# A retention layer with two feed-forward layers: side work at the turn placed by a table, a block of layer 2 written as a sequence of steps

## The chip, the cores and the metric

The kernel runs on one core of a Trainium2 chip. The metric is the time of one execution on the device in microseconds (us). Three runs of the kernel before took 824.14, 824.81 and 824.89 us, a median of 824.81 us.

## What is computed

The reference is a retention attention (scores with a decay, no softmax), whose output is the input of a first feed-forward layer with a leaky rectifier and of a second one with an ELU:

```python
scores = q @ k.transpose / sqrt(64)            # 4 batches, 8 heads, 576 positions, 64 wide
x = (scores * Dmat) @ v                        # Dmat: gamma ** (i - j) for i >= j
x = x.reshape(2304, 512)
h = x @ moe_w_in                               # 512 -> 2048
x = np.maximum(0.01 * h, h) @ moe_w_out        # 2048 -> 512
h = x @ moe2_w_in
g = np.where(h > 0.0, h, np.exp(np.minimum(h, 0.0)) - 1.0)
return g @ moe2_w_out                          # (2304, 512), all float32
```

## The kernel before, in words

**Precision.** TensorE works on float32r operands. A float32 value is kept as a high part (ScalarE copies it to float32r) and a low part (value minus high part, a subtraction on VectorE, "DVE", or GpSimd, "POOL"), and a product is the sum of three: high by high, low by high, high by low. The weights arrive as 64-bit words and are rounded in the kernel. `split_a` issues two ScalarE ("ACT") passes, `split_b` (its generator is `split_ops`, lines 370 to 377) four DVE passes and then the next weight load, `split_c` the high part on ACT (line 388) and the low part on POOL or DVE (line 390). `raw` tiles are what arrives, `u` and `last` the words in work, `wih`, `wil`, `woh`, `wol` the parts of input and output weights.

**Tiling.** The 2304 tokens are four blocks of 512 and a small one of 256. The 2048 inner features are handled in four rounds q of four tiles of 128. Layer 1 is a list of 72 units n, one for a block, a round and one tile (the small block: two tiles). Unit n computes h on PE (`moe_h`, tag `ps_h`, four banks of PSUM), its activation in high and low part (`gh`, `g` on ACT, lines 432 and 433, `gl` on DVE, line 439; in the small block lines 462 to 477), and, three units later (`LAG`), the product with the output weights (`moe_y`, four banks `ps_y`). After a block's last tile of a round, `evac` (line 579, four DVE adds into `yp`; lines 522 and 523 for the small block) empties the four `ps_y` banks. The next block's `moe_y` writes the same four banks. The last round is n = 54 to 71; blocks 0 and 1 are emptied at n = 60 and 64, the small block at n = 66, block 2 at n = 70, block 3 inside layer 2.

**The turn.** Layer 2 computes its first product of a 512-token block by a scheme with seven half-size products instead of eight (`seventh`, numbered 1 to 7), for which the block's output is first turned into sums and differences (`stage`, a generator with nine calls of `side()`): seven ACT high parts (line 642), seven low parts (line 646), four to five DVE differences `t` (line 650), four stores to a scratch in HBM (line 656, `x<-xs`). `load_x` (line 689, `xo<-x`) reads them back as operands. Two of the four weight tiles of a round need sums of their own (`sums_a`: four POOL additions, lines 702 to 705; `sums_b`: line 714 on ACT, 715 on POOL, into `ws`). In the kernel before the place of all this is set by several rules in the loop over n: `begin(n)` and `may_split` start roundings in front of `moe_h`, `held`, `sums_a`, `sums_b`, and `load_x` stand at fixed n, and `side()` is called twice a unit.

**Layer 2.** `seven` is one 512-token block: the products in the order 1, 2, 5, 3, 6, 7, 4, sums of them on DVE (`add_up`, `c`, line 849) with copies on ACT (`copy_of`, `cc`, line 854), four ELU pieces (`elu`: ACT 747 and 749, DVE 751, high part ACT 755, low part DVE 757, into `gg`), one or two weight roundings, and at four places (`spot`) a fourth of an earlier block's output product (`second_y`). Round 0 is emptied by ACT (line 577), the later ones by DVE (line 579). `head = blk == 0` has an order of its own by conditions. The small block is `small_h` and `small_y`.

All engines take their instructions in the written order: this kernel is scheduled by hand. DMAs are issued by SP, in order too, each behind its waits.

Of the kernel before, what the change touches and what calls it, by code (L numbers as in the profile page):

```python
# [10 lines left out]
F32 = mybir.dt.float32  # L11
# [80 lines left out]
def retention_moe(  # L92
# [245 lines left out]


    sources = {"i": [w1_in, w2_in], "o": [w1_out, w2_out]}  # L340
    weights, raws, words = {}, {}, {}

    def load_w(key):
        kind, i = key
# [35 lines left out]
    def split_c(key):  # L380

        u = words[key]
        if key[0] == "o" or key[1] < FT:
# [228 lines left out]
        if loads:  # L612
            load_w(loads.pop(0))

    second = ("i", FT + 2)

    def may_split(n):

        if not splits or splits[0] not in raws or splits[0] == second:
            return False  # L620
        kind, i = splits[0]
        if i >= FT and n >= 63:
            return False
        return i < WB or last_use[kind, min(i, FT + 1) - WB] <= n + (kind == "i")


# [3 lines left out]
    def stage(blk):  # L630

        a = yp.pop(blk)
        n = SIZES[blk] // 2
# [48 lines left out]
        yield from pair(3, t4)  # L682
        yield
        send(3)
# [23 lines left out]
    def sums_b(key):  # L708
        i = key[1]
        for j in (i, i + 1):  # L710
            del words["i", j]
        t = sums[i]
        w = xpool.tile([P, 2, 4, DM // 2], F32R, tag="x", name="ws")
        nc.scalar.activation(w[:, 0], t, AF.Copy)
        nc.gpsimd.tensor_tensor(w[:, 1], t, w[:, 0].bitcast(F32), ALU.subtract)
        sums[i] = w
# [145 lines left out]
            go(steps)  # L862
        over.clear()

    def seven(q, blk, room, rounds, keep, side, begun=None):

        n = SIZES[blk] // 2
        to = (blk + 1) % NMAIN if (q, blk) != (NQ - 1, NMAIN - 1) else None  # L870
        r = list(rounds) + [None] * (2 - len(rounds))
        head = blk == 0
        g = []

        def fetch(k):
            if to is not None and (q, to) != (0, NMAIN - 1):
                load_x(to, k)

        finish()
        fetch(0)  # L880
        a = bank("h", 4)
        seventh(a, q, blk, 0, True)
        p1 = copy_of(a)
        if r[0]:
            split_a(r[0])
        b = bank("h", 4)
        seventh(b, q, blk, 1, True)
        fetch(1)
        c11 = add_up(b, p1)
        z = bank("h", 4)  # L890
        seventh(z, q, blk, 2, True)
        p5 = copy_of(z)
        e11 = elu(c11, g, 0, slice(0, n))
        go(e11, 2)
        if r[0]:
            split_b(r[0])
            load_next()
        spot()
        side()
        g.append(room())  # L900
        go(e11, 1)
        if r[1]:
            split_a(r[1])
        go(e11, 1)
        if begun:
            sums_b(begun)
        seventh(z, q, blk, 3)
        fetch(2)
        p53 = copy_of(z)
        seventh(a, q, blk, 4)  # L910
        c12 = add_up(a, p53)
        go(e11)
        side()
        if r[0] and not keep and not head:
            split_c(r[0])
        e12 = elu(c12, g, 0, slice(n, 2 * n))
        go(e12, 2)
        rest = split_ops(r[1]) if r[1] else iter(())
        if not head:
            go(rest, 3)  # L920
            go(e12, 1)
        spot()
        side()
        if r[0] and head:
            split_c(r[0])
        if not head:
            go(e12, 1)
        seventh(a, q, blk, 5)
        fetch(3)
        c22 = add_up(a, p5)  # L930
        go(e12, 1 + head)
        e22 = elu(c22, g, 1, slice(n, 2 * n))
        go(e22, 2)
        if not head:
            go(rest)
        go(e12)
        spot(2 if head and q > 0 else 1)
        go(rest)
        if r[1]:
            load_next()  # L940
        if r[1] and not keep:
            split_c(r[1])
        side()
        g.append(room())
        go(e22, 1)
        seventh(a, q, blk, 6)
        e21 = elu(a, g, 1, slice(0, n))
        go(e21, 2)
        go(e22, 1)
        go(e21, 1)  # L950
        over.extend((e22, e21))
        pending.append(second_y(q, blk, g))
        spot()

    with tc.manual_schedule():
        qk, v, k = slice(0, 2), slice(2, 3), slice(3, 4)
# [73 lines left out]
            while stages and next(stages[0], end) is end:  # L1030
                stages.popleft()

        held = [("i", FT + 2), ("i", FT + 3)]
        for n, u in enumerate(units):
            p = units[n - LAG] if n >= LAG else None
            if n == B * NMAIN:
# [10 lines left out]
            if n > 2:  # L1047
                begin(n)
            elif n == 0:
                att_q(nxt)  # L1050
# [1 line left out]
            moe_h(u)  # L1052
            for key in rounded:
                split_c(key)
            if n in (69, 70):
                split_c(held[n - 69])
            if rounded == [("i", FT + 1)]:
                sums_a(("i", FT))
            if n == 58:
                sums_b(("i", FT))  # L1060
            side()
            if n == 0:
                att_a(nxt, "h", 4)
                for a in range(1, B):
# [24 lines left out]
            side()  # L1089
            if n > 69:  # L1090
                side()
            for key, at in zip(held, (63, 64)):
                if n == at:
                    assert splits.pop(0) == key
                    split_a(key)
                elif n == at + 1:
                    split_b(key)
                    load_next()
            if n == 65:
                sums_a(held[0])  # L1100
            if n == 70:
                sums_b(held[0])
            if n in (66, 67, 71):
                load_x(0, (66, 67, 71).index(n))

        def first_y(p):
            moe_y(p)
# [7 lines left out]
        def room():  # L1115
            return hpool.tile([P, 2, 2, DM], F32R, tag="gg", name="gg")

        def last_block():
            yield
            yield from stage(NMAIN - 1)  # L1120

        load_x(0, 3)
        stages.append(last_block())
        for q in range(NQ):
            for blk in range(NB):
                if blk < NMAIN:
                    rounds = [splits.pop(0) for _ in range(min(2, len(splits)))]
                    held = rounds if blk == NMAIN - 1 else []
                    seven(q, blk, room if (q, blk) != (0, 0) else big_room, rounds, bool(held), side, begun if held else None)
# [94 lines left out]
```

## Time and profile before

| | |
|---|---|
| median of three runs | 824.81 us |
| profiled execution | 824.94 us |
| its span | 823.2 us |
| around the span | 1.7 us |
| TensorE clock granted, mean | 0.995 |
| PE busy in the span | 802.7 us, 98% |
| DVE, ACT, POOL busy | 531.7, 442.5, 178.7 us |
| layer 1, last round (n = 54 to 71) | about 343 to 445 us |
| layer 2, rounds 0 to 3 | from about 445 us |

PE is the engine that is nearly always busy. The idle time of the others is no loss by itself; the places to look at are those at which PE waits, and the clock that it is granted there.

### The profile page before, as it was taken

What the parts mean: (1) busy time and instruction counts of PE and PEld (TensorE: products, weight loads), DVE (VectorE), ACT (ScalarE), POOL (GpSimd) and SP (SyncE); (2) the same over time, 40 slices, a digit from 0 to 9 for tenths busy, and PEclk for the clock granted to TensorE, in tenths of its full rate; (3) what the DMA queues carried; (4) which work ended last, traced back from release to release, by engine and by line L of the source; (5) the groups of instructions that cost most, each with busy time, mean ns of one, the idle gap of its engine ahead of it and who ended that gap; (6) DMA issues with size and microseconds to landing.
All of it is one profiled execution on the core that took longest, in us unless ns stands there. A gap on an engine that the chain in (4) does not pass through costs nothing.

```text
span 823.2 us, 13324 instructions
## 1 busy us (share of the span) xinstructions
PE 802.7 (98%) x5240; PEld 712.9 (87%) x5240; DVE 531.7 (65%) x861; ACT 442.5 (54%) x755; POOL 178.7 (22%) x160
## 2 busy tenths in 40 slices
PE   9889999999999999999899999999999999999998
PEld 6778888888888888888678879889999999999997
DVE  5998952575244762678765677647776787666544
ACT  3466534554244532555535587777665676555442
POOL 2566431000000000032354123321133112320000
PEclk9999999999999999999899999999999999999999
DMA  9994520122000220122474976726653566545612
GB/s 340 323 335 139 191 78 14 51 78 78 1 25 26 77 77 1 51 76 85 173 261 176 385 277 256 245 76 268 235 218 137 200 263 246 187 131 179 227 53 77
DMA packets 34094, 129.97 MB, mean 158 GB/s; under 512 B 4080, under 2 KB 7408, under 8 KB 26736
## 3 DMA queue, kind: packets, MB, share of 16 engines
q1 hardware_dynamic: 33744, 128.99, 43.8%
q8 instruction: 41, 0.67, 0.3%
q14 instruction: 21, 0.17, 0.1%
q10 hardware_dynamic: 288, 0.14, 0.1%
HBM read 109.71 MB, written 19.40 MB: 157 GB/s over the span
## 4 chain that ended last, share of the span: by engine, by line
PE 37%; DVE 5%; ACT 5%; DMA 3%; issue 1%; POOL 1%; SPq 0%; DVEq 0%; ACTq 0%
PE ps_y L409 20%; PE ps_h L409 17%; DMA xo<-x 2%; DVE gg L757 1%; ACT cc L854 1%; ACT u L358 1%; DVE yp L579 1%; ACT last L360 1%; ACT gg L755 1%; DMA x<-xs 1%; DVE xs L646 1%; DVE t L751 0%; DMA raw<-in_moe_in 0%; DVE u L375 0%; ACT t L747 0%
## 5 line engine op out<-in xcount | busy, mean ns | idle before, releaser
L409 PE MATMUL ps_y<-woh,gg 128*128 128x512 f32 x580 | 183.8, 379 | 0.7 <-ACT yp L577 0.6
L439 DVE TENSOR_TENSOR gl<-g,gh 128x512 fp32r<-128x512 f32 x64 | 46.5, 726 | 133.5 <-ACT g L433 133.2
L409 PEld LDWEIGHTS ps_y<-woh,gg 128*128 128x128 f32 x580 | 109.5, 189 | 15.0 <-ACT yp L577 1.2
L432 ACT ACTIVATE gh<-ps_h 128x512 fp32r<-128x512 f32 x64 | 38.1, 596 | 147.6 <-PE ps_h L409 147.6
L409 PE MATMUL ps_y<-gh,woh 128*128 128x512 f32 x288 | 112.1, 389 | 5.1 <-DVE yp L579 3.9
L409 PE MATMUL ps_y<-gl,woh 128*128 128x512 f32 x288 | 110.3, 383 | 0.0
L409 PE MATMUL ps_y<-wol,gg 128*128 128x512 f32 x290 | 109.5, 378 | 0.0
L409 PE MATMUL ps_y<-gh,wol 128*128 128x512 f32 (+1 forms) x288 | 106.4, 370 | 0.7 <-POOL wol L390 0.7
L409 PE MATMUL ps_h<-xh,wil 128*128 128x512 f32 x256 | 97.3, 380 | 1.9 <-POOL wil L390 1.9
L409 PE MATMUL ps_h<-xh,wih 128*128 128x512 f32 x256 | 97.7, 382 | 1.3 <-ACT wih L388 1.1
L409 PEld LDWEIGHTS ps_h<-xo,ws 128*128 128x128 f32 x720 | 85.8, 192 | 6.6 <-ACT cc L854 2.8
L409 PE MATMUL ps_h<-xo,ws 128*128 128x256 f32 x720 | 88.5, 276 | 3.0 <-DMA xo<-x 1.6
L390 POOL TENSOR_TENSOR wil<-u,wih 128x512 fp32r<-128x512 f32 x20 | 25.7, 1289 | 295.4 <-ACT wih L388 295.3
L849 DVE TENSOR_TENSOR c<-ps_h,cc 128x512 f32<-128x512 f32 x48 | 33.1, 689 | 58.3 <-PE ps_h L409 41.0
L409 PEld LDWEIGHTS ps_y<-gh,woh 128*128 128x128 f32 x288 | 55.0, 191 | 15.1 <-issue 6.5
L409 PE MATMUL ps_h<-xo,wih 128*128 128x256 f32 x360 | 65.3, 275 | 1.5 <-DVE c L849 1.5
L409 PE MATMUL ps_h<-xl,wih 128*128 128x512 f32 x256 | 65.7, 379 | 0.0
L409 PEld LDWEIGHTS ps_y<-gh,wol 128*128 128x128 f32 x288 | 55.1, 191 | 8.2 <-POOL wol L390 1.1
L409 PEld LDWEIGHTS ps_y<-gl,woh 128*128 128x128 f32 x288 | 55.1, 191 | 7.2
L579 DVE TENSOR_TENSOR yp<-yp,ps_y 128x512 f32<-128x512 f32 x96 | 59.6, 680 | 2.4 <-PE ps_y L409 2.4
L755 ACT ACTIVATE gg<-t 128x512 fp32r<-128x512 f32 x64 | 39.9, 625 | 37.4 <-DVE t L751 35.5
L409 PEld LDWEIGHTS ps_y<-wol,gg 128*128 128x128 f32 x290 | 55.0, 190 | 5.7
(119 smaller groups left out, 1522.7 us busy)
## 6 DMA issues: line engine op xcount, KB each, us to landing
xo<-x SPq DMA_DIRECT2D x45, 1024.0 KB, 6.8
raw<-in_moe_in SPq DMA_DIRECT2D x32, 512.0 KB, 3.6
raw<-in_moe_out SPq DMA_DIRECT2D x32, 512.0 KB, 3.5
x<-xs SPq DMA_DIRECT2D x12, 1024.0 KB, 4.5
ain<-in_att SPq DMA_DIRECT2D x16, 512.0 KB, 7.0
xo<-x SPq DMA_DIRECT2D x15, 512.0 KB, 6.2
ain<-in_att SPq DMA_DIRECT2D x20, 256.0 KB, 7.3
out<-yp SPq DMA_DIRECT2D x17, 256.0 KB, 2.1
```

Source lines behind the costliest of these rows:

```text
L358: nc.scalar.activation(u, high.bitcast(F32), AF.Abs, scale=2.0**16)
L360: nc.scalar.activation(last, low, AF.Copy, scale=2.0**-29)
L390: engine.tensor_tensor(l, u, h.bitcast(F32), ALU.subtract)
L409: nc.tensor.matmul(out, w, x, **flags)
L432: nc.scalar.activation(gh, h, AF.Prelu, alpha=0.01)
L439: nc.vector.tensor_tensor(gl, g, gh.bitcast(F32), ALU.subtract)
L579: nc.vector.tensor_tensor(t, t, y[e], ALU.add)
L646: by.tensor_tensor(kept[k][:, i, 1], x, kept[k][:, i, 0].bitcast(F32), ALU.subtract)
L755: nc.scalar.activation(hi, t, AF.Copy)
L757: nc.vector.tensor_tensor(lo, t, hi.bitcast(F32), ALU.subtract)
L849: nc.vector.tensor_tensor(t, x, y, ALU.add)
L854: nc.scalar.activation(t, x, AF.Copy)
```

## The change

The loop over the units gets a table `turn` for n = 54 to 71 with three places a unit: ahead of `moe_h`, behind it, and behind `moe_y`. A token is a step: `a`, `b`, `c` are the three parts of a weight's rounding, `p` and `w` are `sums_a` and `sums_b`, `s` is one `side()`, `x` one `load_x`. The roundings' order is a new list `late`. The low parts of `stage` are all on DVE, and so are those of the two output weights in `early`. A block of layer 2 is a string of tokens, in three kinds: `turn` for round 0, `head` for block 0 of the later rounds, `regular` for the rest (`P` a product, `f` a `load_x`, `k` a copy, `c` an addition, a digit one step of that ELU piece, `aa`, `ba`, `da` the parts of the first rounding and `ab`, `bb`, `db` of the second, `y` a `spot`, `s` a `side()`).

```diff
-        engine = nc.gpsimd if key[1] < FQ or key[1] >= FT else nc.vector
+        engine = nc.gpsimd if key[1] < FQ or key[1] >= FT and key not in early else nc.vector
...
-    late = [("o", FT - 2), ("o", FT - 1), ("o", FT), ("o", FT + 2)]
-    at = order.index(late[0])
-    order = [k for k in order[: at + 6] if k not in late] + late + order[at + 6 :]
+    early = [("o", FT), ("o", FT + 2)]
+    late = "i16 i17 o14 o15 i18 i19 o16 o18"
...
         def low(k, i, x):
-            by = nc.gpsimd if i == 0 else nc.vector
-            by.tensor_tensor(kept[k][:, i, 1], x, kept[k][:, i, 0].bitcast(F32), ALU.subtract)
+            nc.vector.tensor_tensor(
+                kept[k][:, i, 1], x, kept[k][:, i, 0].bitcast(F32), ALU.subtract
+            )
...
+    ORDER = {
+        "regular": (
+            "f0 P1 k1 aa P2 f1 c1 P5 k5 1 1 ba ba ba ba y ga 1 ab 1 w P3 f2 k3 P6 c2 1 da 2 2 bb "
+            "bb 2 y 2 P7 f3 c3 2 3 3 bb 2 y bb db gb 3 P4 4 4 3 4 go y"
+        ),
...
+        "head": (
+            "f0 P1 k1 P2 f1 c1 P5 k5 1 1 aa ba ba y 1 ga P3 f2 k3 P6 c2 1 1 2 2 ba ba 2 y 2 ab P7 "
...
+        turn = {
...
+            62: ("bi19", "", "s pi18"),
+            63: ("", "", "s ao16"),
+            64: ("bo16", "co16", "s s"),
...
-        def last_block():
-            yield
-            yield from stage(NMAIN - 1)
-
-        load_x(0, 3)
-        stages.append(last_block())
+        stages.append(stage(NMAIN - 1))
```

The order of PE's instructions is the same in both kernels. What moves is on the others.

DVE, from the small block's last unit (n = 63) to the emptying of block 1 (line 579), where `xs` are low parts of block 0, `t` differences and `hs`, `gh`, `gl` the small unit's. Before:

```order
L463 TENSOR_TENSOR hs<-hs,ps_h 128x256 x2
L477 TENSOR_TENSOR gh<-hs,gh 128x256
L477 TENSOR_TENSOR gl<-hs,gl 128x256
L646 TENSOR_TENSOR xs<-t,xs 128x512
L650 TENSOR_TENSOR t<-yp,t 128x512
L439 TENSOR_TENSOR gl<-g,gh 128x512
L579 TENSOR_TENSOR yp<-yp,ps_y 128x512 x4
```

Now the same stretch begins behind the small unit's `gh` and `gl`:

```order
L645 TENSOR_TENSOR xs<-t,xs 128x512
L645 TENSOR_TENSOR xs<-yp,xs 128x512
L651 TENSOR_TENSOR t<-yp,t 128x512
L651 TENSOR_TENSOR t<-yp 128x512
L370 TENSOR_SCALAR raw<-raw 128x512
L372 TENSOR_SCALAR u<-u 128x512
L375 SCALAR_TENSOR_TENSOR u<-u,raw 128x512
L377 ISA u<-u,last 128x1024
L439 TENSOR_TENSOR gl<-g,gh 128x512
L390 TENSOR_TENSOR wol<-u,woh 128x512
L579 TENSOR_TENSOR yp<-yp,ps_y 128x512 x4
```

Behind the small unit DVE has a low part, a difference and `gl` ahead of the four adds before, and two low parts, two differences, a rounding (370 to 377), `gl` and an output weight's low part now.

ACT, the same place, before (299 is `stage`, 358 and 360 `split_a`, 432 and 433 the activation of n = 64):

```order
L462 ACTIVATE hs<-ps_h 128x256 x2
L466 ACTIVATE hs<-hs 128x512
L476 ACTIVATE gh<-hs 128x256
L476 ACTIVATE gl<-hs 128x256
L642 ACTIVATE xs<-t 128x512
L358 ACTIVATE u<-raw 128x512
L360 ACTIVATE last<-raw 128x512
L432 ACTIVATE gh<-ps_h 128x512
L433 ACTIVATE g<-ps_h 128x512
```

Now:

```order
L462 ACTIVATE hs<-ps_h 128x256 x2
L466 ACTIVATE hs<-hs 128x512
L476 ACTIVATE gh<-hs 128x256
L476 ACTIVATE gl<-hs 128x256
L358 ACTIVATE u<-raw 128x512
L360 ACTIVATE last<-raw 128x512
L432 ACTIVATE gh<-ps_h 128x512
L433 ACTIVATE g<-ps_h 128x512
L388 ACTIVATE woh<-u 128x512
```

The high part of line 642, which needs a difference from DVE, has left the front of `gh`. Two passes of a rounding stand there in both, of another weight now, and the high part of that weight (line 388) follows the activation.

DVE in block 1 of round 0, from the addition behind product 6 to that behind product 7 (both line 849, now 852). Before:

```order
L849 TENSOR_TENSOR c<-ps_h,cc 128x512
L757 TENSOR_TENSOR gg<-t,gg 128x2x256
L646 TENSOR_TENSOR xs<-yp,xs 128x512
L650 TENSOR_TENSOR t<-yp 128x512
L370 TENSOR_SCALAR raw<-raw 128x512
L372 TENSOR_SCALAR u<-u 128x512
L375 SCALAR_TENSOR_TENSOR u<-u,raw 128x512
L751 SCALAR_TENSOR_TENSOR t<-t,c 128x512
L849 TENSOR_TENSOR c<-ps_h,cc 128x512
```

Now:

```order
L852 TENSOR_TENSOR c<-ps_h,cc 128x512
L760 TENSOR_TENSOR gg<-t,gg 128x2x256
L370 TENSOR_SCALAR raw<-raw 128x512
L372 TENSOR_SCALAR u<-u 128x512
L754 SCALAR_TENSOR_TENSOR t<-t,c 128x512
L852 TENSOR_TENSOR c<-ps_h,cc 128x512
```

The low part and the difference of `stage` and the third pass of the rounding have left the stretch between the two additions.

## Rows read from the trace of the kernel before

**Rows 1.** The page's first part: busy us (share) and instructions.

```profile
PE 802.7 (98%) x5240; PEld 712.9 (87%) x5240; DVE 531.7 (65%) x861; ACT 442.5 (54%) x755; POOL 178.7 (22%) x160
```

**Rows 2.** PE's waits, 380 to 560 us: us in total, times, longest.

```profile
PE ps_y L409 <- DVE yp L579: 3.9, 1, 3.9
PE ps_h L409 <- DVE c L849: 1.8, 2, 1.5
PE ps_h L409 <- DMA xo<-x: 1.6, 1, 1.6
PE ps_h L409 <- ACT cc L854: 1.4, 3, 0.7
PE ps_y L409 <- DVE yp L523: 1.0, 1, 1.0
PE ps_y L409 <- ACT yp L577: 0.6, 3, 0.2
```

**Rows 3.** Windows: busy PE, PEld, DVE, ACT, POOL; PEclk; DMA share; GB/s.

```profile
405.00:410.00 5.00, 2.85 (x9) 2.52 (x10) 4.29 (x7) 2.48 (x6) 1.28 (x1) 0.61 0.40 161
410.00:415.00 5.00, 5.00 (x20) 4.30 (x19) 4.90 (x9) 2.73 (x6) 0.00 (x0) 0.71 0.56 206
...
560.00:600.00 40.00, 40.00 (x270) 37.42 (x269) 30.35 (x51) 27.58 (x46) 6.40 (x6) 1.00 0.72 270
```

**Rows 4.** Timeline before the wait at 407 us: start, us, engine, operation, [idle].

```profile
398.63 0.64 ACT L462 ACTIVATE hs<-ps_h 128x256 f32<-128x256 f32 x2
...
401.27 0.42 DVE L477 TENSOR_TENSOR gl<-hs,gl 128x256 fp32r<-128x256 f32 x1
...
404.61 0.58 ACT L432 ACTIVATE gh<-ps_h 128x512 fp32r<-128x512 f32 x1
...
405.71 0.69 DVE L439 TENSOR_TENSOR gl<-g,gh 128x512 fp32r<-128x512 f32 x1 [2.82 <-ACT g L433]
406.32 2.47 DVE L579 TENSOR_TENSOR yp<-yp,ps_y 128x512 f32<-128x512 f32 x4
...
407.15 0.77 PE L409 MATMUL ps_y<-gh,woh 128*128 128x512 f32 x1 [3.93 <-DVE yp L579]
```

**Rows 5.** Timeline of DVE: first and last of a rounding's four passes.

```profile
389.07 0.53 DVE L370 TENSOR_SCALAR raw<-raw 128x512 uint32<-128x512 uint32 x1
...
390.83 0.69 DVE L377 CUSTOM_DVE_ANT_0 u<-u,last 128x1024 uint16<-128x1024 uint16 x1
```

**Rows 6.** Timeline: DVE low part and difference beside POOL work.

```profile
385.70 1.76 DVE L646 TENSOR_TENSOR xs<-yp,xs 128x512 fp32r<-128x512 f32 x1
...
416.68 1.19 POOL L703 TENSOR_TENSOR sum<-u 128x256 f32<-128x256 f32 x1
...
418.34 1.22 DVE L650 TENSOR_TENSOR t<-yp,t 128x512 f32<-128x512 f32 x1
```

**Rows 7.** Timeline of block 0, layer 2, round 0: SP, ACT and PE.

```profile
449.00 3.08 SPq L689 DMA_DIRECT2D xo<-x  x4
...
452.26 0.60 ACT L854 ACTIVATE cc<-ps_h 128x512 f32<-128x512 f32 x1
...
456.08 1.60 PE L409 MATMUL ps_h<-xo,ws 128*128 128x256 f32 x12 [1.56 <-DMA xo<-x]
```

**Rows 8.** Timeline of DVE in block 1 of round 0.

```profile
480.24 1.78 DVE L757 TENSOR_TENSOR gg<-t,gg 128x512 fp32r<-128x512 f32 x1
...
481.94 0.68 DVE L646 TENSOR_TENSOR xs<-yp,xs 128x512 fp32r<-128x512 f32 x1
...
485.35 0.68 DVE L849 TENSOR_TENSOR c<-ps_h,cc 128x512 f32<-128x512 f32 x1
```

**Rows 9.** Timeline of a block of round 1: DVE and ACT at its end.

```profile
578.17 2.47 DVE L579 TENSOR_TENSOR yp<-yp,ps_y 128x512 f32<-128x512 f32 x4
...
580.26 0.60 ACT L747 ACTIVATE t<-ps_h 128x512 f32<-128x512 f32 x1 [1.35 <-PE ps_h L409]
...
584.20 0.60 ACT L854 ACTIVATE cc<-ps_h 128x512 f32<-128x512 f32 x1 [1.29 <-PE ps_h L409]
```

More of the change, by code (lines that the diff above doesn't have):

```diff
@@ L340, in retention_moe @@
     sources = {"i": [w1_in, w2_in], "o": [w1_out, w2_out]}
-    weights, raws, words = {}, {}, {}
+    weights, raws, words, added = {}, {}, {}, set()
     def load_w(key):
@@ L599, in retention_moe @@
     ]
-    late = [("o", FT - 2), ("o", FT - 1), ("o", FT), ("o", FT + 2)]
-    at = order.index(late[0])
-    order = [k for k in order[: at + 6] if k not in late] + late + order[at + 6 :]
+    early = [("o", FT), ("o", FT + 2)]
+    late = "i16 i17 o14 o15 i18 i19 o16 o18"
+    late = [(k[0], int(k[1:])) for k in late.split()]
+    at = order.index(("o", FT - 2))
+    order = order[:at] + late + order[at + 8 :]
     loads, splits = list(order), list(order)
@@ L613, in load_next @@
             load_w(loads.pop(0))
-    second = ("i", FT + 2)
     def may_split(n):
-        if not splits or splits[0] not in raws or splits[0] == second:
+        if not splits or splits[0] not in raws:
             return False
         kind, i = splits[0]
-        if i >= FT and n >= 63:
-            return False
         return i < WB or last_use[kind, min(i, FT + 1) - WB] <= n + (kind == "i")
@@ L632, in stage @@
         a = yp.pop(blk)
+        assert blk not in yb
         n = SIZES[blk] // 2
@@ L710, in sums_b @@
         for j in (i, i + 1):
-            del words["i", j]
+            added.add(("i", j))
+            if ("i", j) in weights:
+                del words["i", j]
         t = sums[i]
@@ L863, in finish @@
         over.clear()
-    def seven(q, blk, room, rounds, keep, side, begun=None):
+    ORDER = {
[3 more added lines that the diff above has]
+        ),
+        "turn": (
+            "f0 P1 k1 aa P2 f1 c1 P5 k5 1 1 ba ba ba ba y s ga 1 ab 1 w P3 f2 k3 P6 c2 1 da 2 2 "
+            "bb bb 2 y 2 P7 f3 c3 2 3 3 bb 2 y bb db s s gb 3 P4 4 4 3 4 go y s"
+        ),
+        "head": (
+            "f0 P1 k1 P2 f1 c1 P5 k5 1 1 aa ba ba y 1 ga P3 f2 k3 P6 c2 1 1 2 2 ba ba 2 y 2 ab P7 "
+            "f3 c3 3 3 2 y y da bb bb bb bb db gb 3 w P4 4 4 3 4 go y"
+        ),
+    }
@@ L869, in seven, with operand @@
+    def seven(kind, q, blk, room, rounds, keep, side, begun=None):
         n = SIZES[blk] // 2
         to = (blk + 1) % NMAIN if (q, blk) != (NQ - 1, NMAIN - 1) else None
[L871 to L875, printed above, removed]
+        lower, upper = slice(0, n), slice(n, 2 * n)
+        slabs = dict(zip("ab", rounds))
+        g, banks, copies, acts, ops = [], {}, {}, {}, {}
+        def operand(x):
             if to is not None and (q, to) != (0, NMAIN - 1):
-                load_x(to, k)
@@ L879, in seven @@
-        finish()
[L880 to L953, printed above, removed]
+                load_x(to, x)
+        def seventh_of(x):
+            at = {2: "b", 5: "z", 3: "z"}.get(x, "a")
+            if x in (1, 2, 5):
+                banks[at] = bank("h", 4)
+            seventh(banks[at], q, blk, (1, 2, 5, 3, 6, 7, 4).index(x), x in (1, 2, 5))
+            if x == 4:
+                acts[4] = elu(banks["a"], g, 1, lower)
@@ new lines, in seven @@
+        finish()
+        for token in ORDER[kind].split():
+            op, x = token[0], token[1:]
+            if op == "P":
+                seventh_of(int(x))
+            elif op == "f":
+                operand(int(x))
+            elif op == "k":
+                copies[x] = copy_of(banks["a" if x == "1" else "z"])
+            elif op == "c":
+                y = add_up(banks["b" if x == "1" else "a"], copies.pop({"1": "1", "2": "3", "3": "5"}[x]))
+                acts[int(x)] = elu(y, g, int(x) // 3, lower if x == "1" else upper)
+            elif op in "1234":
+                go(acts[int(op)], 1)
+            elif token == "go":
+                pending.append(second_y(q, blk, g))
+            elif op == "g":
+                g.append(room())
+            elif op == "a" and x in slabs:
+                split_a(slabs[x])
+                ops[x] = split_ops(slabs[x])
+            elif op == "b" and x in slabs:
+                if next(ops[x], end) is end:
+                    load_next()
+            elif op == "d" and x in slabs and not keep:
+                split_c(slabs[x])
+            elif op == "w" and begun:
+                sums_b(begun)
+            elif op == "y":
+                spot()
+            elif op == "s":
+                side()
@@ L955, in retention_moe @@
+        over.extend(acts[x] for x in (3, 4))
     with tc.manual_schedule():
@@ L1031, in side, with act @@
                 stages.popleft()
-        held = [("i", FT + 2), ("i", FT + 3)]
+        TURN = 54
+        turn = {
+            54: ("", "", "ai16"),
+            55: ("bi16", "ci16", ""),
+            56: ("", "", "ai17"),
+            57: ("bi17", "ci17 pi16", "ao14"),
+            58: ("bo14", "co14 wi16", "ao15"),
+            59: ("bo15", "co15", "ai18"),
+            60: ("bi18", "", "s"),
+            61: ("", "s", "ai19"),
+            62: ("bi19", "", "s pi18"),
+            63: ("", "", "s ao16"),
+            64: ("bo16", "co16", "s s"),
+            65: ("", "s", "s ao18"),
+            66: ("bo18", "co18", "s s"),
+            67: ("", "s", "s wi18 x0"),
+            68: ("", "s", "s x1"),
+            69: ("", "ci18 s", "s"),
+            70: ("", "ci19", "s s x2"),
+            71: ("", "s s", "s s x3"),
+        }
+        def act(n, k):
+            for token in turn.get(n, ("", "", ""))[k].split():
+                op, key = token[0], (token[1:2], int(token[2:] or 0))
+                if op == "s":
+                    side()
+                elif op == "x":
+                    load_x(0, int(token[1:]))
+                elif op == "a":
+                    assert splits.pop(0) == key
+                    split_a(key)
+                elif op == "b":
+                    split_b(key)
+                    load_next()
+                else:
+                    {"c": split_c, "p": sums_a, "w": sums_b}[op](key)
         for n, u in enumerate(units):
@@ L1054, in retention_moe @@
                 split_c(key)
[L1055 to L1061, printed above, removed]
+            act(n, 1)
             if n == 0:
@@ L1088, in retention_moe @@
                 stages.append(stage((60, 64, 70).index(n)))
[L1089 to L1104, printed above, removed]
+            act(n, 2)
         def first_y(p):
@@ L1126, in retention_moe @@
                 if blk < NMAIN:
+                    kind = "turn" if q == 0 else "head" if blk == 0 else "regular"
                     rounds = [splits.pop(0) for _ in range(min(2, len(splits)))]
                     held = rounds if blk == NMAIN - 1 else []
-                    seven(q, blk, room if (q, blk) != (0, 0) else big_room, rounds, bool(held), side, begun if held else None)
+                    seven(kind, q, blk, room if (q, blk) != (0, 0) else big_room, rounds, bool(held), side, begun if held else None)
                     if (q, blk) == (0, 0):
```

5 lines of the change are left out of this document (3 added, 2 removed).

## The prediction

> **What bounds the kernel now.** I read the page's first part, then PE's waits by stretch, then the windows with the granted clock, and last the timeline of each place that stood out. PE is busy for 802.7 of 823.2 us [rows 1]; a change that leaves the order of its instructions as it is can win only its idle time and its slow clock. Where are these? Between 380 and 560 us PE waits 3.9 + 1.8 + 1.6 + 1.4 + 1.0 + 0.6 = 10.3 us for other engines and one DMA [rows 2]. From 560 us on it is full: 40.00 of 40 us [rows 3]. Most of the other idle time is at the start, which the diff does not touch. And there is the clock: in the ten microseconds from 405 the granted clock averages 0.61 and 0.71, so its lower level (1.2 GHz) held for (0.39 + 0.29) x 5 / 0.5 = 6.8 us: 3.9 us of the first window, of which PE was busy for 2.85, and 2.9 us of the second [rows 3]. 5.75 us of work at half speed is 2.9 us lost. Before it PE had waited 3.9 us; the mean granted clock over the span, 0.995, leaves less than a microsecond for all other places, so no wait of 1.6 us or less was followed by a fall. 10.3 + 2.9 = 13.2 us can be won, and 824.94 - 13.2 = 811.7 us is the floor.
>
> **The wait at 407 us and the clock (3.9 + 2.9 us).** PE needs the four `ps_y` banks of block 1, which the four adds of line 579 empty. They stand on DVE behind `gl` (405.71), this behind `gh` on ACT (404.61) [rows 4]. PE had come to the wait at 407.15 - 3.93 = 403.2, so the `h` that `gh` reads was done a whole unit earlier. ACT was late because it took the small block's `hs` only at 398.63, and a high part of `stage` and a rounding stood between. The small unit's chain runs from 398.63 to 401.69, 3.1 us [rows 4].
> For the changed kernel I count from PE. Between the end of that small `h` and the wait lie two units of 24 matmuls of 512 columns, 2 x 24 x 512 / 2.4 GHz = 10.2 us, so it ends at 393.0 on the old time axis. ACT then holds nothing that waits for a late difference. The chain takes 3.1 us (to 396.1). Now come two low parts and two differences, 4 x 0.69 = 2.8 us (a subtraction of two SBUF tiles like `gl` in [rows 4]; 398.9), a rounding, 389.07 to 391.52, 2.5 us [rows 5] (401.4), `gl` and an output weight's low part, 1.4 us (402.8), and the first add, a quarter of 2.47 us [rows 4] (403.4). PE asks at 403.2. DVE instructions that follow each other overlap by about a tenth (four adds take 2.47 us, not 4 x 0.69), which takes some 0.6 us off. So the banks come between 0.4 us early and 0.2 us late, and the clock has no reason to fall. This one place decides 6.8 of the 13.2 us, and it is close.
>
> **Low parts on DVE.** Each stage moves four low parts from POOL to DVE, and two output weights' go too: 18 x 0.69 = 12.4 us more for an engine that is busy for 65% [rows 1]. In exchange DVE keeps its short times: beside POOL a low part took 1.76 us [rows 6]. Those in the chain are counted above; elsewhere DVE's idle time hides them.
> Against it: POOL is not silent. `sums_a` of the second pair moves from n = 65 to n = 62, into the front of this chain. Beside such sums a difference took 1.22 us instead of 0.69 [rows 6], 0.5 us for each of four sums: between 0 and 2.1 us, of which all is covered that falls ahead of 393. I take 0.6 us, nearer to nothing, because the four sums follow DVE's work of n = 62, a unit early.
> The Trainium skill ("SBUF — State Buffer", Who interferes with whom) says that a DVE instruction with two SBUF inputs and a GpSimd instruction that reads SBUF shut each other out for a whole instruction. By that rule each of the four sums, 1.19 us long in the row, could hold DVE for its whole length, 4.8 us together; the row shows 0.5 us lost for one.
>
> **The small block's banks (1.0 us).** PE asks for these two units later, 10.2 us after it asked for block 1's. Ahead of them DVE has four adds (2.5), three low parts and a difference (2.8), two `gl` and a weight's low part (2.1), a rounding (2.5): 9.9 us at full durations, about 9 with the overlap, and the first pair of half-size adds. Gone, with less than a microsecond to spare.
>
> **Block 0 of round 0 (1.6 us, and a part of the copies' 1.4).** Product 6 waits for its operand until 456.08; SP issued that load only in a row that begins at 449.00 [rows 7], behind a store that waited for late low parts. Now it stands in the table at n = 70, ahead of block 2's stores. It lands within 456.08 - 449.00 = 7.1 us, and from n = 70 to product 6 lie a unit and a half and four products, over 12 us: hidden. Product 3 waits for the copy that ends at 452.86 [rows 7], up to 0.7 us [rows 2]. On ACT it stands behind high parts that wait for DVE's differences; with the low parts at their short times, 1.1 us less each, these come earlier by more than that.
>
> **Block 1 of round 0 (1.5 us), blocks 2 and 3.** The second addition starts at 485.35 [rows 8], and PE waits 1.5 us for it [rows 2]. Between 481.94 and it stand a low part, a difference, three rounding passes and an ELU step. The low part, the difference and the third pass go behind it: 0.68 + 0.69 + 0.6 (a quarter of [rows 5]) = 2.0 us, more than 1.5. The 1.78 us at 480.24 [rows 8], beside POOL, stays. In block 3 only the pass goes, 0.6 us against a wait of 0.3 (1.8 - 1.5, [rows 2]). The three waits of 0.2 us for ACT's line 577 [rows 2] follow from these additions, behind which ACT takes its ELU steps: gone.
>
> **Block 0 of round 1.** The third of the waits for a copy is here: two ACT passes of a rounding stood between the copies of products 1 and 5 and now follow both. Gone; later heads did not wait.
>
> **Regular blocks.** One real change: the third rounding pass goes behind the ELU step and the fourth behind the emptying of an output, 2.47 us [rows 9]. The second weight's high part on ACT follows it, some 3 us later, and the copies of the next block behind that. ACT has 1.35 + 1.29 us idle just there [rows 9], and the copy that PE waits for, that of product 5, is due 2 x 12 x 256 / 2.4 GHz = 2.6 us after the first. Cost: nothing; without this cover up to 3.1 us (the emptying and a pass) in each of six blocks of rounds 1 and 2. Round 3 has no roundings.
>
> **Sum.** 13.2 us less 1.0 us that I leave standing (0.6 for POOL's sums, 0.4 for the close calls at the two emptyings) is 12.2 us: 824.94 - 12.2 = 812.7 us. The profiled execution is 0.13 us above the median, so the same holds for it.
>
> **Rivals.**
> *POOL's sums hit the chain at n = 62 to 64.* For: the 1.76 and 1.22 us in [rows 6], and a slack of half a microsecond. Against: they come a unit before. Price: all four sums at 0.5 us instead of the 0.6 taken, 1.5 us, the clock stays: 814.2; up to 816 if the next emptying is hit too. By the rule quoted, with 4.8 us, it would be the next rival.
> *The wait stays as long as it was*, since DVE now carries all low parts ahead of the adds, and the clock falls again. For: 2.8 + 2.5 + 1.4 us of DVE behind a chain of 3.1 are 9.8 of 10.2 us. Against: the same count. 3.9 + 2.9 us come back: 812.7 + 6.8 - 0.6 = 818.9.
> *Slower*: the fourth rounding pass behind the emptying. If ACT's high part, and with it ELU steps and copies, delays product 3 by the whole 3.1 us in six blocks, that is 18.6 us: 831.3. It decides from 12.2 / 6 = 2.0 us a block on. For: ACT takes its work in order. Against: its idle time in [rows 9].
> *No gain*: each wait handed to the next late bank, which needs several of these at once.
>
> **Chances.** Forecast, 811.5 to 813.8: 0.62. First rival, to 816.5: 0.18. Second, to 820: 0.11. Slower: 0.06. No gain: 0.03. Below the floor only the runs' own spread (0.4 us) leads. 811.2 to 818.0 leaves out less than 0.2. What a measurement of this kernel can tell from no change is about 0.2%, 1.6 us: faster 0.91, within 0.03, slower 0.06.
>
> **What would show it.** First step: the 3.93 us row gone, and a granted clock of 1.00 in all windows from 400 to 450. Blocks: no PE wait for `xo<-x`, a copy or an addition in round 0. PE waits after 550 us would say that the regular order costs. If PE still waits for block 1's banks, see whether DVE's small-unit rows run beside POOL's sums. I am wrong if PE's idle time only moves, to n = 54 to 60 for instance, where I expect none.

## The result and the profile after

The changed kernel takes 811.12 us (median of four runs, 808.98 to 811.35) against 824.49 us for the kernel before (four runs, 824.14 to 824.89) in the same comparison: ratio 0.9832, 95% interval 0.9814 to 0.9850. The forecast was 812.7 us with a range from 811.2. So the direction and the places were right, and the time lies 0.08 us below the lowest that I had allowed: 13.4 us won in place of 12.2, where I had put the most that could be won at 13.2.

The page's first part, busy us (share) and instructions, answers to [rows 1]:

```profile
PE 795.8 (99%) x5240; PEld 711.2 (88%) x5240; DVE 535.6 (66%) x879; ACT 444.3 (55%) x755; POOL 156.0 (19%) x142
```

PE is busy for 6.9 us less with the same 5240 instructions: these are the slow matmuls of [rows 3], the first matmuls behind waits, which are longer, and the last ones in front of waits, whose ends the next matmul otherwise overlaps. The span fell from 823.2 to 807.2 us. POOL's 22.7 us less and DVE's 18 instructions more are the low parts.

PE's waits of the profiled execution (808.98 us) from 360 us to the end; the six rows of [rows 2] are all gone, and one stands ahead of that stretch, near 377 us:

```profile
PE ps_y L409 <- ACT woh L388: 0.3, 1, 0.3
```

The windows of [rows 3] in the same execution (busy PE, PEld, DVE, ACT, POOL; PEclk; DMA share; GB/s). The granted clock, 0.61 and 0.71 before, is 1.00, its upper level (2.4 GHz), in both:

```profile
405.00:410.00 5.00, 5.00 (x29) 4.50 (x28) 4.81 (x9) 3.07 (x6) 0.00 (x0) 1.00 0.87 358
410.00:415.00 5.00, 5.00 (x28) 4.48 (x27) 4.67 (x11) 2.13 (x6) 1.17 (x2) 1.00 0.69 211
560.00:600.00 40.00, 40.00 (x271) 37.45 (x270) 30.03 (x46) 25.96 (x42) 10.13 (x8) 1.00 0.59 224
```

The timeline of the turn, which answers to [rows 4] (start, us, engine, operation, [idle before]):

```profile
390.54 0.73 POOL L703 TENSOR_TENSOR sum<-u 128x256 f32<-128x256 f32 x1 [16.03 <-DVE u L377]
...
392.73 0.80 POOL L706 TENSOR_TENSOR sum<-u,sum 128x256 f32<-128x256 f32 x1
392.85 0.95 DVE L477 TENSOR_TENSOR gl<-hs,gl 128x256 fp32r<-128x256 f32 x1
...
393.42 0.83 ACT L462 ACTIVATE hs<-ps_h 128x256 f32<-128x256 f32 x2
...
396.19 0.42 DVE L477 TENSOR_TENSOR gl<-hs,gl 128x256 fp32r<-128x256 f32 x1
...
399.05 0.60 ACT L432 ACTIVATE gh<-ps_h 128x512 fp32r<-128x512 f32 x1 [1.38 <-PE ps_h L409]
...
402.81 2.48 DVE L579 TENSOR_TENSOR yp<-yp,ps_y 128x512 f32<-128x512 f32 x4
...
403.17 1.03 PE L409 MATMUL ps_h<-xl,wih 128*128 128x512 f32 x4
...
404.03 0.38 PE L409 MATMUL ps_y<-gh,woh 128*128 128x512 f32 x1
```

ACT's `gh` waits for PE now and not for DVE, the adds of line 579 start 1.22 us ahead of the matmul that needs the first of them, and this matmul follows the one before it without a wait. POOL's sums end at 393.53 (392.73 and 0.80), as the chain of the small unit begins (393.42).

**How the two traces are laid beside each other.** PE's instructions are the same and in the same order, so the k-th of one trace can be set against the k-th of the other, and each step of the difference between their starts is time won or lost at that place. The sums by starts below come from this; no view of one trace alone shows them.

### The profile page after: what moved, and what is told of

Its sections match the earlier page's. It is cut to its first block, busy times and chain, and to the rows that moved or that the text cites. A ratio compares the mean times of both kernels' runs of the same rounds, so it can differ in the third digit from the quotient of the medians.

```text
span 807.2 us, 13312 instructions
## 1 busy us (share of the span) xinstructions
PE 795.8 (99%) x5240; PEld 711.2 (88%) x5240; DVE 535.6 (66%) x879; ACT 444.3 (55%) x755; POOL 156.0 (19%) x142
## 4 chain that ended last, share of the span: by engine, by line
PE 88%; DMA 3%; issue 3%; DVE 2%; POOL 1%; ACT 1%; SPq 0%; DVEq 0%; POOLq 0%; ACTq 0%
PE ps_y L409 44%; PE ps_h L409 41%; DMA ain<-in_att 2%; PE ps_h L214 1%; PE ps_h L260 1%; DMA raw<-in_moe_out 1%; DMA kn<-in_att 1%; PE ps_h L307 0%; PE ps_h L272 0%; DVE raw L370 0%; POOL wil L390 0%; DVE ain L232 0%; DVE u L377 0%; DVE xt L291 0%; ACT u L358 0%
## 5 line engine op out<-in xcount | busy, mean ns | idle before, releaser
L439 DVE TENSOR_TENSOR gl<-g,gh 128x512 fp32r<-128x512 f32 x64 | 44.7, 699 | 117.4 <-ACT g L433 117.2
L358 ACT ACTIVATE u<-raw 128x512 f32<-128x512 f32 x64 | 54.0, 844 | 9.9 <-DMA raw<-in_moe_in 6.6
```

The costliest lines, as they stand in the source:

```text
L358: nc.scalar.activation(u, high.bitcast(F32), AF.Abs, scale=2.0**16)
L439: nc.vector.tensor_tensor(gl, g, gh.bitcast(F32), ALU.subtract)
```

## The experiments

**The changed kernel again** (`after_again`, no edit).

> The changed kernel once more, for a second trace and more times. Theory A (the gain is the waits and the slow clock of the turn and of round 0, each wait costing some tenths of a us more than its row shows, nothing else): the same 16 us against the trace of before, place by place, and between 809 and 811.5 us. Theory B (a part of the gain is not at those places but at the start or in rounds 1 to 3, and comes and goes from run to run): where this run differs from the first one by more than 1 us, the difference lies outside 380 to 560 us.

811.54 us (810.91 to 811.69), ratio 0.9833 (0.9815 to 0.9851). With the first four, seven of eight runs lie at 810.9 to 811.7 and one, the profiled one above, at 808.98. PE's waits in this second profiled execution (810.91 us), 360 to 820 us:

```profile
PE ps_h L409 <- DVE c L852: 1.1, 2, 0.7
PE ps_y L409 <- ACT woh L388: 0.4, 1, 0.4
PE ps_y L409 <- DVE yp L579: 0.3, 1, 0.3
```

The two executions go side by side to 449.6 us; then the second loses 1.0 us at product 7 of block 0, round 0, 0.5 at 456 us and 0.4 at product 7 of block 1. So it is 14.0 us ahead of the trace of before and not 16, and its median lies just above the range of theory A; theory B is out, since the whole difference lies at these three places. ACT shows why. First the execution of 808.98 us, then that of 810.91 us:

```profile
444.87 0.63 ACT L642 ACTIVATE xs<-t 128x512 fp32r<-128x512 f32 x1 [1.05 <-DMA x<-xs]
...
447.26 0.58 ACT L857 ACTIVATE cc<-ps_h 128x512 f32<-128x512 f32 x1
...
449.64 1.50 PE L409 MATMUL ps_h<-xo,ws 128*128 128x256 f32 x12
```

```profile
446.59 0.63 ACT L642 ACTIVATE xs<-t 128x512 fp32r<-128x512 f32 x1 [2.73 <-DMA x<-xs]
...
449.20 0.57 ACT L857 ACTIVATE cc<-ps_h 128x512 f32<-128x512 f32 x1
...
450.55 1.60 PE L409 MATMUL ps_h<-xo,ws 128*128 128x256 f32 x12 [0.71 <-DVE c L852]
```

A high part of `stage` (line 642) waits for the store that frees its buffer. Behind it in ACT's row stands the copy `cc`, which the addition `c` and with it product 7 needs. With 1.05 us of waiting that is hidden; with 2.73 us it is not. Why the store lands later is open: SP issues its stores at the same times in both executions to 0.1 us, but between 435 and 440 us the DMAs move 338 GB/s in the first and 186 in the second.

**One half of the change at a time** (`turn_only`: the table and the low parts on DVE, with the block code of before; `seven_only`: the three sequences, with the unit loop, the order of roundings and the low parts of before).

```diff
# turn_only, against the changed kernel
-        for token in ORDER[kind].split():
...
+        if not head:
+            go(rest, 3)
+            go(e12, 1)
+        spot()
+        side()
# seven_only, against the kernel before
-    def seven(q, blk, room, rounds, keep, side, begun=None):
+    def seven(kind, q, blk, room, rounds, keep, side, begun=None):
```

> The table of the turn, the order of roundings and all low parts on DVE, with the old sequence of a layer 2 block (one empty call of side() first, as before). Theory A: the waits ahead of layer 2 stay gone (by the aligned traces 7.6 us with the clock, of 16) and so does the wait for the DMA in block 0 (1.8 us); the waits for copies and additions in round 0 and in block 0 of round 1 come back (about 5.5 us in all): 815 to 817 us. Theory B: less than 4 us come back, since these waits were themselves made by the late stages.

> The new sequences of a layer 2 block on the old turn, low parts on POOL as before. Theory A: the wait of 3.9 us for block 1's banks and the clock's fall, the small block's wait and the DMA's in block 0 stay; the waits for additions in blocks 1 and 3, for the copy in block 0 of round 1 and for ACT's line 577 go: 4 to 5.5 us faster than before, 819 to 820.5 us. Theory B (the sequence does not matter, the late stages make the waits): under 2 us faster.

`turn_only` 818.27 us (817.29 to 819.51), 1 to 3 us over what I expected; `seven_only` 819.57 us (819.28 to 819.94), as expected. They won 6.5 and 5.2 us of the 13.2 us that the whole change won against the same runs of before (824.74 us); the rest needs both halves. PE's waits from 360 us on, of `turn_only`:

```profile
PE ps_h L409 <- DVE c L852: 3.6, 2, 2.6
PE ps_h L409 <- ACT cc L857: 1.6, 2, 1.2
PE ps_y L409 <- ACT woh L388: 0.3, 1, 0.3
PE ps_y L409 <- DVE yp L579: 0.3, 1, 0.3
PE ps_y L409 <- ACT yp L577: 0.2, 1, 0.2
```

of `seven_only`:

```profile
PE ps_y L409 <- DVE yp L579: 3.9, 1, 3.9
PE ps_h L409 <- DMA xo<-x: 1.5, 1, 1.5
PE ps_y L409 <- DVE yp L523: 1.2, 1, 1.2
PE ps_h L409 <- ACT cc L854: 1.1, 2, 0.7
```

The table removes the wait at 407 us, the small block's, and block 0's DMA wait; the sequences remove the additions' waits, those for line 577 and the copy's in block 0 of round 1. The miss of `turn_only` lies in round 0: with the old block code behind the new table the addition's wait in block 1 was not 1.5 us [rows 2] but 2.6, the copy's there 1.2 and not 0.2, product 7 of block 0 waited 1.0 us for its addition, and the clock fell behind the wait of 2.6 us (1.4 us more by the starts), as this window of `turn_only` shows (0.50 is the lower level, 1.2 GHz):

```profile
482.00:484.00 2.00, 2.00 (x8) 1.78 (x8) 0.53 (x1) 2.00 (x5) 0.00 (x0) 0.50 0.62 262
```

**The first low part of each pair back on POOL** (`lows_pool`).

```diff
-            nc.vector.tensor_tensor(
+            by = nc.gpsimd if i == 0 else nc.vector
+            by.tensor_tensor(
```

> The changed kernel with the stages' first low part of each pair back on POOL (the two output weights' stay on DVE). Theory A (the order of ACT and DVE ahead of the emptying decides; slack for it is 0.6 us): DVE has one instruction less in each pair but is held up by POOL for about 1 us, so block 1's banks come about at the same time; at most 1 us of waits returns and the clock stays up: within 1 us of the changed kernel. Rival (low parts on DVE are what keeps DVE on time): a wait of 1 us or more ahead of n = 65, another at the small block, 2 to 7 us slower.

811.45 us (810.35 to 812.24), ratio 0.9831 (0.9808 to 0.9854): no difference from the changed kernel that these runs can show, and in its profile PE waits neither ahead of n = 65 nor for the small block's banks. So the rival is out. On which of the two engines the first low part of a pair of `stage` runs does not matter once the rest stands in the right place; the two output weights' low parts were not moved back.

**More work on DVE ahead of block 1's adds** (`lows_rep2`, `lows_rep4`, `lows_rep5`: the two low parts that stand ahead of them done two, four and five times, the output unchanged).

```diff
-                low(k, i, x)
+                for _ in range(REP if (blk, k) == (0, 1) else 1):
+                    low(k, i, x)
```

> The changed kernel with VectorE's two low parts ahead of block 1's emptying done twice: 1.2 us more on VectorE ahead of the adds that PE waits for near 404 us, where they were 0.6 us early. Theory A (a wait costs its row and some tenths): a row of 0.6 us and 0.7 to 1.0 us by the starts of PE's instructions. Theory B (a wait costs its row): a row of 0.6 us and 0.6 us. No fall of the clock by either. Theory C (the slack is larger than read): nothing.

> The same low parts four times: 3.6 us more on VectorE. By the slack of 0.6 us a row of 3.0 us for PE near 404 us; theory A 3.1 to 3.4 us by the starts, theory B 3.0. Open is whether TensorE's clock falls behind it: 3.9 us was followed by the lower level in the kernel before, 1.6 us was not. If it falls, some 2.8 us more behind it (5.9 to 6.2 together), if not, none.

> The changed kernel with the two low parts ahead of block 1's emptying done five times: one repetition more than in the run whose wait of 3.6 us left the clock at its upper level. VectorE is 1.2 us later, so PE's row there should be 4.8 us and its start 5.0 us late. Theory A (the lower clock of the kernel before was the answer to PE's standing still, here 3.9 us): the granted clock falls to 0.5 for some 7 us behind the wait and 2.8 us more are lost, 7.8 us together by the starts. Theory B (the lower clock came from something else in the kernel before): clock 1.00 and 5.0 us.

One execution each: 813.37, 815.60 and 818.70 us. PE and the adds at the place, in the order of the three kernels (lines 411 and 581 are 409 and 579, moved by the edit):

```profile
403.50 1.03 PE L411 MATMUL ps_h<-xl,wih 128*128 128x512 f32 x4
...
404.69 2.47 DVE L581 TENSOR_TENSOR yp<-yp,ps_y 128x512 f32<-128x512 f32 x4
...
405.52 0.46 PE L411 MATMUL ps_y<-gh,woh 128*128 128x512 f32 x1 [0.99 <-DVE yp L581]
```

```profile
402.79 1.03 PE L411 MATMUL ps_h<-xl,wih 128*128 128x512 f32 x4
...
406.60 2.47 DVE L581 TENSOR_TENSOR yp<-yp,ps_y 128x512 f32<-128x512 f32 x4
...
407.43 0.46 PE L411 MATMUL ps_y<-gh,woh 128*128 128x512 f32 x1 [3.62 <-DVE yp L581]
```

```profile
403.55 1.03 PE L411 MATMUL ps_h<-xl,wih 128*128 128x512 f32 x4
...
408.75 2.48 DVE L581 TENSOR_TENSOR yp<-yp,ps_y 128x512 f32<-128x512 f32 x4
...
409.58 0.77 PE L411 MATMUL ps_y<-gh,woh 128*128 128x512 f32 x1 [5.00 <-DVE yp L581]
```

Two things follow. First, the price of a wait. Without one the second of these rows starts 0.86 us after the first (403.17 and 404.03 in the changed kernel); here it starts 2.02, 4.64 and 6.03 us after it. So the losses are 1.16, 3.78 and 5.17 us, each 0.16 to 0.17 us more than its row, because the row counts from the end of a group that lasts 1.03 us, while the next group normally starts 0.17 us before that end. The next matmul is late by some 0.1 us more. My theory A (the row and some tenths) holds in kind, but the losses for two and four repetitions (0.7 to 1.0 and 3.1 to 3.4 us expected) were larger, for two reasons. The slack, 0.6 us in the expectation, is smaller: where PE waited for the adds, it started 0.83 us after they did (406.32 and 407.15 in [rows 4]), so the changed kernel's 1.22 us leave 0.39. And the adds came later than expected: set against the first of PE's rows, they start 1.55, 4.17 and 5.56 us later than in the changed kernel (402.81 and 403.17), where 1.2, 3.6 and 4.8 were expected. Less 0.39 these are the three losses.

Second, the clock. The windows around the wait of `lows_rep4`, and of `lows_rep5`:

```profile
405.00:410.00 5.00, 2.57 (x15) 2.41 (x16) 4.91 (x9) 2.64 (x5) 0.00 (x0) 1.00 0.82 269
```

```profile
405.00:410.00 5.00, 0.42 (x1) 0.45 (x2) 4.74 (x10) 2.52 (x5) 0.00 (x0) 0.76 0.38 84
410.00:415.00 5.00, 5.00 (x18) 4.31 (x18) 4.90 (x10) 2.03 (x4) 0.00 (x0) 0.56 0.93 379
```

With the wait of 5.00 us the clock fell and PE lost 2.4 us more by its starts; with 3.62 us it did not. It fell while PE still stood: 0.76 over 405 to 410 us is 2.4 us at the lower level, from 407.6 on, and the wait ended at 409.58. In the kernel before it fell inside the wait of 3.93 us too, at 406.1 by the 3.9 us that the prediction reads from [rows 3], and in `turn_only` just behind one of 2.62 us. That a long wait of PE can bring the lower level with it was my reading, and `lows_rep5` bears it out; its length alone does not say whether.

**ACT's high part out of the way** (`turn0`: in block 0 of round 0 the first `s` stands behind the addition that product 7 needs; `turn0_w`: besides, the rounding of the column sums two units later).

```diff
+        "turn0": (
+            "f0 P1 k1 aa P2 f1 c1 P5 k5 1 1 ba ba ba ba y ga 1 ab 1 w P3 f2 k3 P6 c2 1 s da 2 2 "
...
# turn0_w besides
-            58: ("bo14", "co14 wi16", "ao15"),
+            58: ("bo14", "co14", "ao15"),
...
-            60: ("bi18", "", "s"),
+            60: ("bi18", "wi16", "s"),
```

> The changed kernel with one side step of block 0 moved: ScalarE's high part of stage 2's last pair stands behind the copy and the addition ahead of product 7 instead of in front of the copy. In the run of 807.2 us that copy waited 1.05 us for the store of the buffer, in the one of 809.1 us 2.73 us, and all PE groups from product 7 on are late by the difference. Theory A (the landing of that store is what makes the 811 us runs): the waits for the addition in blocks 0 and 1 of round 0 go, 808.8 to 809.6 us in every run, ratio about 0.981. Theory B (the 2 us come from somewhere else, and ScalarE's wait is a symptom): 810.9 to 811.7 us as the changed kernel, with the wait for the addition still there. Theory C (the high part that comes later makes the store and so the operands of block 1 late): 811.5 to 814 us and a PE wait for a loaded operand near 455 to 470 us.

> As the run before, and ScalarE's rounding of the first column sums (1.1 us, ahead of the weight that PE waited 0.35 us for near 378 us) is put two units later. If a wait costs its row and a few tenths: 0.3 to 0.6 us less than the run before, and no wait on woh at 378 us. If another instruction takes its place: the same as the run before.

`turn0` 808.83 us (808.40 to 809.64, five runs), ratio 0.9811 (0.9797 to 0.9824); `turn0_w` 808.39 us (807.63 to 808.61, four runs), ratio 0.9806 (0.9793 to 0.9819). Theory A holds: the runs are now at the level that one of eight had. ACT in `turn0`, the copy ahead of the high part, which no longer waits:

```profile
447.06 0.58 ACT L857 ACTIVATE cc<-ps_h 128x512 f32<-128x512 f32 x1
447.54 0.62 ACT L642 ACTIVATE xs<-t 128x512 fp32r<-128x512 f32 x1
```

In `turn0`'s profile PE still waits 0.4 us for `woh` near 378 us; in that of `turn0_w` PE has no wait at all from 360 us on. The high part of that weight on ACT, in the changed kernel and in `turn0_w`:

```profile
376.99 0.63 ACT L388 ACTIVATE woh<-u 128x512 fp32r<-128x512 f32 x1 [2.46 <-DVE u L377]
```

```profile
374.08 0.63 ACT L388 ACTIVATE woh<-u 128x512 fp32r<-128x512 f32 x1 [0.75 <-DVE u L377]
```

It comes 2.9 us earlier. The wait was a close one: the profiles of `lows_rep2` and `head_old`, with the table as it was, have no row of it either. The difference of the medians, 0.44 us, fits a wait of 0.35 to 0.4 us but is no larger than the spread of the runs. `turn0_w` has the lowest median here, and all its runs lie below all eight of the changed kernel; from `turn0` its runs do not tell it.

**The later rounds' sequences, one at a time** (`reg_old`: the rounding passes of `regular` where they were; `head_old`: block 0 of rounds 1 to 3 in the order of before).

```diff
# reg_old
-            "bb 2 y 2 P7 f3 c3 2 3 3 bb 2 y bb db gb 3 P4 4 4 3 4 go y"
+            "bb bb 2 y 2 P7 f3 c3 2 3 3 bb 2 y db gb 3 P4 4 4 3 4 go y"
# head_old
-            "f0 P1 k1 P2 f1 c1 P5 k5 1 1 aa ba ba y 1 ga P3 f2 k3 P6 c2 1 1 2 2 ba ba 2 y 2 ab P7 "
+            "f0 P1 k1 aa P2 f1 c1 P5 k5 1 1 ba ba ba ba y ga 1 ab 1 w P3 f2 k3 P6 c2 1 2 2 y da P7 "
```

> The changed kernel with the regular sequence's rounding passes where they were before: the third ahead of the activation's third step, the fourth ahead of the emptying in place of behind it. Theory A (regular blocks have no wait on PE in either order, the passes are cover only): within 0.5 us of the changed kernel's 811.3, PE's starts from 560 us on the same to 0.3 us. Theory B (the passes' new place gives part of the gain of the later rounds): 0.5 to 1.5 us slower, with waits for yp or c in blocks 1 to 3 of the later rounds.

> The changed kernel with block 0 of rounds 1 to 3 in the order of before (first slab's rounding passes between products 5 and 3, the second copy and the activation of product 6 behind them). Theory A: the wait for the copy near 541 us in round 1 comes back, a row of 0.5 us and by the starts 0.5 to 1.1 us, and 0.3 us near 660 us in round 2; the median 0.7 to 1.3 us above the changed kernel's 811.3, ratio about 0.985. Theory B (the gain in round 1 comes from what the turn left over, not from the order): within 0.3 us.

`reg_old` 812.10 us (810.16 to 814.78; ratio 0.9844, 0.9818 to 0.9870): its runs spread too widely to show half a microsecond, but in its profile PE has no wait from 380 us on, and PE's starts keep their distance from the changed kernel's to 0.1 us from 500 us to the end. In this execution the regular order neither costs nor gives. `head_old` 812.05 us (810.75 to 812.45; ratio 0.9835, 0.9816 to 0.9855): by the medians not to be told from the changed kernel, by the trace yes. Its waits, 360 to 820 us:

```profile
PE ps_h L409 <- DVE c L852: 1.7, 2, 1.4
PE ps_h L409 <- ACT cc L857: 0.5, 1, 0.5
PE ps_y L409 <- DVE yp L579: 0.3, 1, 0.3
```

The first row is product 7 of blocks 0 and 1 of round 0, as in the second execution of the changed kernel. The copy's wait is back, and by the starts it costs 0.75 us at 538 us and 0.3 at 543; nothing comes back in rounds 2 and 3 but 0.06 us. What I expected there, 0.3 us in round 2, is not this order's.

## Where the prediction was right, and the step that failed

**The step that failed is the sum of the first paragraph**: "10.3 + 2.9 = 13.2 us can be won, and 824.94 - 13.2 = 811.7 us is the floor." It rests on the sentence that the change "can win only its idle time and its slow clock", and so it priced each wait by its row. The places are right and complete but for two of 0.3 us; the price of each was too low. Set against `turn0_w`, which has no wait there, the kernel before loses 16.79 us from 380 us on:

| part, by the starts of PE's instructions | us |
|---|---|
| the 11 waits of [rows 2] by their rows | 10.35 |
| their starts, on top of the rows (11 x 0.16) | 1.73 |
| the matmul behind each, where the clock stays (9 places) | 0.88 |
| the half clock behind 407 us | 2.86 |
| the small block's other three banks, each paced by an add | 0.42 |
| places without a row of a wait, and some that `turn0_w` lost | 0.55 |

So the floor was no higher than 824.94 - 16.8 = 808.1 us, where the forecast had 811.7. (That `turn0_w`'s profiled execution took 808.29 us is no second proof of it: the table was measured against that trace, and the two differ by 0.13 us ahead of 380 us.) The clock's term was right for this execution (2.9 forecast). A wait's row is a lower bound: here a wait cost 0.16 us more than it at its own matmul, and some 0.1 us at the next one where the clock stayed. That the first part of this comes from the wait itself is what `lows_rep2`, `lows_rep4` and `lows_rep5` show. The small block's pacing shows in the kernel before:

```profile
421.63 0.45 PE L409 MATMUL ps_y<-gh,woh 128*128 128x512 f32 x1 [1.01 <-DVE yp L523]
...
422.42 0.45 PE L409 MATMUL ps_y<-gh,woh 128*128 128x512 f32 x1
...
423.20 0.45 PE L409 MATMUL ps_y<-gh,woh 128*128 128x512 f32 x1
```

Each bank begins 0.78 us after the last, where three matmuls back to back take 0.65, and no row calls that a wait.

**What was left standing**: I took 1.0 us, in the wrong places. POOL's sums cost nothing: they ran from 390.54 to 393.53, beside two short DVE instructions of n = 62 that took 0.73 and 0.95 us instead of 0.42, and the chain began as the last sum ended. Nor were the 1.19 us of [rows 6] a sum's own length, on which the 4.8 us were worked out: POOL was held up in that row as well, and the sum before it in that trace took 0.74 us, those here 0.73 to 0.80. The two emptyings were close, as forecast, but cost no time. What did stay is 2.7 us, by the starts of the second profiled execution, whose time is that of most runs: 0.9 at `woh` near 378 us, which the table made new (I expected none there), and some 1.8, net, in blocks 0 to 2 of round 0. The two errors have opposite signs: 3.6 us too little to be won and 1.7 us too little left make 1.9 us, and the time came out 1.6 us under the forecast; the rest lies within the runs' spread. That the forecast came so near is in this part luck.

Point by point:

- **The wait at 407 us**: right, almost to the row. The chain takes 3.2 us (393.42 to 396.61; 3.1 forecast), the adds are 0.39 us early (0.4 early to 0.2 late forecast), and the clock stays up. That it is close was right too: `lows_rep2`, whose adds come 1.55 us later, waits 0.99 us.
- **Low parts on DVE cost nothing**: right (`lows_pool`).
- **The small block's banks**: right; the first pair of adds ends at 413.25 and PE starts on them without a wait.
- **Block 0 of round 0**: the load's wait and the copy's went. But I wrote that the high parts on ACT wait for DVE's differences and come earlier with these. They wait for their buffer too, and once DVE was quick, the store that frees it came last. I had read the load and store queue for the load that PE needed, and not for the stores that ACT's high parts needed.
- **Block 1**: "2.0 us, more than 1.5" was right: product 4's wait for the addition is gone in both profiles. The 0.39 us that product 7 waits in the second is the lateness that block 0 hands on; it is gone in `turn0`.
- **Blocks 2 and 3, and block 0 of round 1**: right; `head_old` brings the last back.
- **Regular blocks cost nothing**: right; PE has no wait from 380 us on in the first profile, and none in that of `reg_old`. The slower rival, 831.3 us, rested on this place alone and fell with it.
- **The rivals on the turn** (814.2 and 818.9): neither came. `lows_rep5` shows of what size the second would have been: a wait of 5.00 us, in place of 3.9, and the lower clock gave 818.70 in one execution.

## What to carry to other kernels

Price a wait of PE from start to start, against a place where the same groups follow each other without one; the row of a wait counts from the end of the last matmul and leaves out part of the loss, which over eleven waits was 2.6 of 16.8 us here. When an engine that made others late becomes quick, list for each instruction behind it everything that it waits for, the buffer among them: here the store that frees a buffer was the next in line. And where PE's instructions keep their order, lay the two traces over each other by instruction number, which here found two microseconds that medians and waits left open.

## What the runs showed that I had not expected

- The clock's fall does not go by the length of the last wait alone: 2.62 us (`turn_only`) and 3.93 us (before) came with the lower level, 3.62 us (`lows_rep4`) did not. What decides between them is open; it was not tried further.
- The 2.9 us of slow clock are those of one profiled execution. Of the 23 runs of the kernel before that stand beside the experiments, nine have a mean granted clock of 0.998, about 3 us at the lower level, and the others 0.994 to 0.997, about 5 to 10 us; their medians, 824.25 and 824.99 us, differ by only 0.7 us. No trace of these runs was kept, so how much of the clock's term is in the median is not shown.
- Ahead of 100 us, where no edit reaches, the profiled executions of the changed kernels differ by up to 1.5 us by the starts of PE's instructions: `turn0` is 1.1 us behind the changed kernel there and `lows_rep4` 0.5 us ahead. A difference of medians smaller than that needs the traces.
- The same program took 808.98 us once and 810.9 to 811.7 us seven times. Between the two executions that were profiled the whole difference hangs on one store: ACT waited 1.05 us for it in the one and 2.73 us in the other. The other six have no profile, but `turn0`, which only takes that wait out of the copy's way, brought all five of its runs to 808.4 to 809.6 us.
- Of the new wait for `woh` near 378 us, 0.35 us by its row, the starts show 0.9 us lost, spread over four matmuls.
